# Reordering a prologue, turning the pass loop of a second product, and moving early weight splits and key/query products from GpSimd to VectorE

## The chip, the core and the metric

The kernel runs on one core of a Trainium2 chip. The metric is the device time of one execution in microseconds (us). One execution is also recorded by the hardware profiler; times "from the start" count from the start of its span. The engines are named as the profile names them: PE (TensorE) with its weight loads PEld, DVE (VectorE), ACT (ScalarE), POOL (GpSimd), and SP, whose queue issues most of the DMAs.

## The reference

What is computed is a gated linear attention over 4 batches, 8 heads, 768 tokens and head size 48, then a mixture of 4 experts over the 3072 tokens, then a gated product layer:

```python
f = 1.0 / (1.0 + np.exp(-f_logit))
for t in range(S):
    state = f[:, :, t, :, None] * state + np.einsum('bhd,bhe->bhde', k[:, :, t], v[:, :, t])
    y[:, :, t] = np.einsum('bhd,bhde->bhe', q[:, :, t], state)
...
p = domain_probs / (domain_probs.sum(-1, keepdims=True) + 1e-09)
for e in range(E):
    h = np.maximum(x @ w1[e], 0.0)
    out += p[:, e:e + 1] * (h @ w2[e])
...
a = x @ w1
b = x @ w2
h = a * b @ w3
return (h @ w_out).astype(np.float32)
```

## The kernel before, in words

**High and low parts.** Matrix products are made in a reduced format (fp32r) three times over: each operand is split into a high part and a low part, and high times high, high times low and low times high are added up in PSUM. `PASSES = ((0, 0), (0, 1), (1, 0))` lists these pairs as (part of the weight, part of the other operand); 0 is high, 1 is low.

**Units.** The expert stage works on pieces called units here: one slice f of 128 of an expert's 1024 hidden features, for one block of tokens. `stage1` makes the hidden slice: nine matmuls into `hps` (L721), the high part of `hid` on ACT (L727), the low part on DVE (L728), which reads ACT's result. `stage2` multiplies the slice with the second weight: nine matmuls into `y` (L755), three output tiles t times three passes; before, t is the outer loop and the pass the inner one. Tile t lies in a PSUM bank of its own. `stage2` of a unit runs after `stage1` of the next. After an expert's last slice DVE multiplies `y` with the gate `pb` (L771, or L774 into `tmp`, which POOL adds to `acc`, L775). The first expert is done on two half blocks of 256 tokens, so units 0 to 15 have matmuls of 256 columns; from unit 16 on they have 512, and 384 in the last layer (the M stage), where no attention is left.

**Weights.** A weight piece of 128 x 768 is loaded by SP into `raw` (L161), copied to the high part of `w` on ACT (L174), and its low part is made on POOL (L175). `feed` does this ahead of the units that need the piece. 160 pieces are split so.

**Attention.** Tokens come in 24 chunks m of 128. Step by step: `a_exp`, `a_add` (gates, L233 and L238 on ACT, from chunk 4 on L240 on DVE), `a_scan` (L245, DVE, into `pi`), `a_ln` and `a_rec` (L253, L257, ACT, into `r`), `a_k` (key times `pi`, L262: DVE for m < 3, else POOL), `a_t` (L268, DVE, on `pi` and `r`), `a_q1` (query times `r`, L275: DVE for m < 3, else POOL), `a_q2` (L279 and L282, DVE), `a_p` (PE: `psk` L311 and `ps` L319; `asb` on DVE, L322), `a_st` and `a_y` (PE: `psy` L343 to L359, `psu` L369), `a_xh` and `a_xl` (L388 on ACT, L392 on DVE: the token block `x` for the experts), and `a_s` (`us` L413 on DVE, `state` L414 on POOL).

**What sets the order.** The order of instructions on each engine is the order in which the program issues them. The prologue is a list written out by hand (`asteps`), with `warm(n)` putting in matmuls whose result nobody reads. The gates of the experts (`gate_`, L131 to L134 on DVE; `gate_rows_`, a transpose `pT` on PE, a copy `pt` on ACT and a store `pdr`) stand in that list; `load_gate(0, 0)` follows the list and reads `pdr` back into `pb`. After it, the steps of later chunks are spread over the units by due times (`plan`).

Of the kernel before, what the change touches and what calls it, by code (L numbers as in the profile page):

```python
# [8 lines left out]
F32 = mybir.dt.float32  # L9
# [3 lines left out]
ALU = mybir.AluOpType  # L13
# [7 lines left out]
PASSES = ((0, 0), (0, 1), (1, 0))  # L21
# [3 lines left out]
def gated_linear_attention_moe_kernel(  # L25
# [16 lines left out]
    nc = tc.nc  # L42
    B, H, S, D = fkq.shape[0], 2 * fkq.shape[1], fkq.shape[4], fkq.shape[2] // 2
    NT, DM = out.shape
    E = w1.shape[0]
# [100 lines left out]
    def load_gate(b, e):  # L146
        t = two.tile([128, CB, 128], F32, tag="pb", name="pb")
        src = pdr[b * CB:(b + 1) * CB, e, :]
        nc.sync.dma_start(out=t, in_=src.unsqueeze(0).to_broadcast([128, CB, 128]))
        pb[b, e] = t  # L150
# [4 lines left out]
    wts = {}  # L155
# [15 lines left out]
    def split_chunk(key, c):  # L171
        raw = raw_q.pop(c)
        w = wp.tile([128, 2, 768], F32R, tag="w", name="w")
        nc.scalar.activation(out=w[:, 0], in_=raw, func=AF.Copy)  # L174
        nc.gpsimd.tensor_tensor(out=w[:, 1], in0=raw, in1=w[:, 0].bitcast(F32), op=ALU.subtract)  # L175
        wts[key] = w


# [79 lines left out]

    def a_k(m, g=ALL):
        pi, k = part(m, "pi", None, g), kq_of(m, 0, g)  # L260
        eng = nc.vector if m < 3 else nc.gpsimd
        eng.tensor_tensor(out=k, in0=k, in1=pi[:, :, 1:], op=ALU.mult)  # L262
        nc.gpsimd.tensor_copy(out=pends[:, m, g[0]:g[1]].unsqueeze(2), in_=pi[:, :, C:])  # L263

# [6 lines left out]

    def a_q1(m, g=ALL):
        r, q = part(m, "r", None, g), kq_of(m, 1, g)
        eng = nc.vector if m < 3 else nc.gpsimd
        eng.tensor_tensor(out=q, in0=q, in1=r, op=ALU.mult)  # L275

    def a_q2(m, g=ALL):
# [199 lines left out]
    def gate_rows_():  # L477
        gate_rows(praw[0])
# [9 lines left out]
        (a_scan, 1, G0), (a_scan, 1, G1), (a_p, 0), (a_ln, 1, G0), (a_rec, 1, G0), (a_ln, 1, G1), (a_rec, 1, G1),  # L488
        (load_f, 1), (load_kq, 1), (load_v, 2), (warm, 5), (a_y, 0), (a_k, 1, G0), (a_t, 1, G0), (a_q1, 1, G0),
        (a_q2, 1, G0), (a_k, 1, G1), (a_t, 1, G1), (a_q1, 1, G1), (a_q2, 1, G1), (a_xh, 0), (a_s, 0), (warm, 5),  # L490
        (a_p, 1), (a_st, 1), (feed_, 1), (a_xl, 0), (warm, 3), (a_y, 1), (a_exp, 2), (a_add, 2), (feed_, 1), (a_scan, 2),
        (gate_,), (a_xh, 1), (a_xl, 1), (gate_rows_,), (a_ln, 2), (a_rec, 2), (a_s, 1), (warm, 5), (a_k, 2), (a_t, 2), (a_q1, 2),
        (a_q2, 2), (feed_, 1),
    ]

    def ahead(m):
# [150 lines left out]
    start = {}  # L647
# [54 lines left out]
    yps = {}  # L702
# [37 lines left out]
    def stage2(i):  # L740
        kind, sb, e, blk, f, t0, t1 = units[i]
        hb = 2 * sb + blk
        nt = t1 - t0
        h = hid.pop(i)
        w = wts[(run_of(sb, e, blk), "2", e, f // 2) if kind == "E" else (sb, "w", 0, f // 2)]
        w = w.rearrange("p l (i c) -> p l i c", i=2)[:, :, f % 2, :]
        f0 = 0 if kind == "E" else e * NF // 2
        f1 = NF - 1 if kind == "E" else (e + 1) * NF // 2 - 1
        for t in range(3):
            if f == f0:  # L750
                yps[t] = ps_y.tile([128, 512], F32, tag=f"y{t}", name="y")[:, 0:nt]
            ts = slice(t * 128, (t + 1) * 128)
            for n, (wl, hl) in enumerate(PASSES):
                lhsT, rhs = (w[:, wl, ts], h[:, hl]) if kind == "E" else (h[:, hl, ts], w[:, wl])
                nc.tensor.matmul(  # L755
                    yps[t], lhsT=lhsT, rhs=rhs, start=(f == f0 and n == 0), stop=(f == f1 and n == 2)
                )
        if f != f1:
            return
        fresh = (kind, hb, t0) not in begun  # L760
        begun.add((kind, hb, t0))
        if fresh and t0 == 0:
            n = TB if kind == "E" else NB
            acc[hb] = accp.tile([128, 3, TB], F32, tag="acc", name="acc")[:, :, 0:n]
        a = acc[hb]
        if kind == "E":
            pe = pb[hb, e].rearrange("p i t -> p (i t)")[:, t0:t1]
            for t in range(3):
                at_ = a[:, t, t0:t1]
                if fresh:  # L770
                    nc.vector.tensor_tensor(out=at_, in0=yps[t], in1=pe, op=ALU.mult)  # L771
                else:
                    tmp = two.tile([128, TB], F32, tag="tmp", name="tmp")[:, 0:nt]
                    nc.vector.tensor_tensor(out=tmp, in0=yps[t], in1=pe, op=ALU.mult)  # L774
                    nc.gpsimd.tensor_tensor(out=at_, in0=at_, in1=tmp, op=ALU.add)  # L775
            if e == E - 1:
                nc.sync.dma_start(out=x2d[:, :, hb * TB:(hb + 1) * TB], in_=a)
        else:
            for t in range(3):
                if e == 0:  # L780
                    nc.scalar.activation(out=a[:, t], in_=yps[t], func=AF.Copy)
                else:
                    nc.vector.tensor_tensor(out=a[:, t], in0=yps[t], in1=a[:, t], op=ALU.add)
                    r0 = hb * NB + t * 128
                    nc.sync.dma_start(out=out[r0:r0 + 128, :], in_=a[:, t])
# [55 lines left out]
    def feed(i, most):  # L841

        nonlocal nload, nsplit
        while nsplit < len(seq):
            while nload < len(seq) and nload < nsplit + RB - 2:
                load_chunk(seq[nload][1:])
                nload += 1
            if not most:
                break
            wb = WB  # L850
            if nsplit >= wb and last_use[seq[nsplit - wb]] >= i:
                break
            split_chunk(seq[nsplit], seq[nsplit][1:])
            nsplit += 1
            most -= 1

    with tc.manual_schedule():
        both = nc.sync, nc.scalar
        load_f(0, (0,), both)
        load_kq(0, (0, 1), both)  # L860
        load_f(0, (1,))
        load_v(0)
        load_kq(0, (1, 2))
        setup()
        praw.append(gate_load())
        feed(0, 0)
        load_v(1)
        warm(24)
        for st in asteps[:PRO]:
            run(st)  # L870
        load_gate(0, 0)
        for i, u in enumerate(units):
            feed(i, 1)
            while any(c not in wts for c in unit_chunks(u)):
                feed(i, 1)
            stage1(i)
            ends = i and units[i - 1][1:4] + units[i - 1][5:] != u[1:4] + u[5:]
            if ends:
                stage2(i - 1)
            half = (len(plan[i]) + 1) // 2  # L880
            for st in plan[i][:half]:
                run(st)
            if i and not ends:
                stage2(i - 1)
            for st in plan[i][half:]:
                run(st)
            kind, sb, e, blk, f = u[:5]
            if kind == "E" and f == NF // 2 and u[6] == TB:
                g = gates.index((2 * sb + blk, e)) + 1
                if g < len(gates):  # L890
                    load_gate(*gates[g])
        stage2(len(units) - 1)
# [221 lines left out]
```

## Time and profile before

| | |
|---|---|
| median of 3 runs | 1290.7 us (1290.09 to 1291.15) |
| the profiled execution | 1291.08 us, its span 1289.4 us |
| mean granted clock of PE over it | 0.993 |
| PE busy | 1260.7 us, 98% of the span |
| DVE busy | 634.9 us, 49% |
| POOL busy | 531.0 us, 41% |
| ACT busy | 427.7 us, 33% |

PE's clock has two levels, 2.4 and 1.2 GHz; a granted clock of 1.00 is the first, 0.50 the second, and a value between them is the mean over a stretch with both. In the rows below, the columns of a timeline are start, duration, engine, line, operation, operands, count, and in brackets the idle time of the engine just before, with what ended it. In a group of instructions they are line, engine, operation, operands, shapes and count, then busy time and mean ns of one, then the idle time before them.

### The profile page before, as it was taken

To read this page: it belongs to the slowest core of one execution; us is meant where nothing else is said; L and a number is where in the kernel's file an instruction comes from. 1 tells how busy PE (TensorE), PEld (TensorE's weight loads), DVE (VectorE), ACT (ScalarE), POOL (GpSimd) and SP (SyncE) were. 2 spreads that over 40 slices of the span, in tenths; PEclk is the share of its full clock that TensorE was granted. 3 is DMA by queue.
4 is the path that set the end of the run, shared out by engine and by line. 5 is a ranking of instruction groups with operands and counts; after the bars stand their busy time and mean duration, and the time that the engine had idled before them with its cause. 6 is when DMAs were issued, how large, how long until landed. Compare 5 with 4: busy or idle time off the path is not lost.

```text
span 1289.4 us, 18213 instructions
## 1 busy us (share of the span) xinstructions
PE 1260.7 (98%) x6935; PEld 1092.9 (85%) x6935; DVE 634.9 (49%) x1035; ACT 427.7 (33%) x760; POOL 531.0 (41%) x413
## 2 busy tenths in 40 slices
PE   7889999999999999999999999999999999999997
PEld 7888888888878888787888778788888999999997
DVE  7654443334465546565336766756624242332422
ACT  5434233342332323232222323324223433443431
POOL 3656345553542516354352635635433222222310
PEclk8989999999999999999999999999999999999999
DMA  7644343542635434252224422414134133231301
GB/s 197 181 146 121 98 133 101 148 125 72 170 115 134 140 105 148 81 156 82 77 80 134 121 80 87 144 56 131 55 99 129 56 94 98 91 104 55 117 1 40
DMA packets 107263, 138.74 MB, mean 108 GB/s; under 512 B 9664, under 2 KB 80672, under 8 KB 107168
## 3 DMA queue, kind: packets, MB, share of 16 engines
q1 hardware_dynamic: 106400, 137.16, 35.9%
q8 instruction: 56, 0.92, 0.3%
q10 hardware_dynamic: 768, 0.34, 0.1%
q14 instruction: 39, 0.32, 0.1%
HBM read 115.39 MB, written 14.20 MB: 101 GB/s over the span
## 4 chain that ended last, share of the span: by engine, by line
PE 88%; DVE 6%; POOL 2%; issue 2%; ACT 1%; DVEq 0%; ACTq 0%; POOLq 0%
PE hps L721 43%; PE y L755 36%; PE wps L634 3%; PE ps L319 2%; PE psy L359 2%; PE psy L343 1%; PE warm L469 1%; POOL w L175 1%; POOL acc L775 1%; PE psu L369 1%; DVE hid L728 1%; DVE dexp L553 1%; DVE pi L268 1%; DVE dexp L552 1%; PE psk L311 1%
## 5 line engine op out<-in xcount | busy, mean ns | idle before, releaser
L721 PE MATMUL hps<-x,w 128*128 128x512 f32 (+2 forms) x2952 | 648.3, 367 | 1.6 <-DVE ab L735 1.3
L721 PEld LDWEIGHTS hps<-x,w 128*128 128x128 f32 x2952 | 532.3, 189 | 75.8 <-DVE ab L735 1.6
L755 PE MATMUL y<-hid,w 128*128 128x512 f32 (+1 forms) x1800 | 443.7, 390 | 11.5 <-DVE hid L728 8.3
L175 POOL TENSOR_TENSOR w<-raw,w 128x768 fp32r<-128x768 f32 x160 | 302.9, 1895 | 293.0 <-ACT w L174 258.5
L755 PEld LDWEIGHTS y<-hid,w 128*128 128x128 f32 x1800 | 327.8, 189 | 88.8 <-DVE hid L728 12.0
L728 DVE SCALAR_TENSOR_TENSOR hid<-hps,hid 128x512 fp32r<-128x512 f32 (+1 forms) x200 | 133.6, 668 | 385.7 <-ACT hid L727 385.6
L727 ACT ACTIVATE hid<-hps 128x512 fp32r<-128x512 f32 (+1 forms) x200 | 115.6, 578 | 392.6 <-PE hps L721 392.5
L174 ACT ACTIVATE w<-raw 128x768 fp32r<-128x768 f32 x160 | 133.8, 837 | 55.2 <-PE y L755 55.2
L735 DVE TENSOR_TENSOR ab<-hps,a 128x384 f32<-128x384 f32 x64 | 35.6, 557 | 164.0 <-PE hps L721 164.0
L572 POOL TENSOR_TENSOR dman<-dman,dexp 128x384 f32<-128x384 f32 (+1 forms) x46 | 46.2, 1004 | 166.5 <-ACT dman L570 142.1
L755 PE MATMUL y<-w,hid 128*128 128x384 f32 x576 | 110.7, 337 | 0.1
L775 POOL TENSOR_TENSOR acc<-acc,tmp 128x512 f32<-128x512 f32 x54 | 71.9, 1361 | 79.0 <-DVE tmp L774 79.0
L755 PEld LDWEIGHTS y<-w,hid 128*128 128x128 f32 x576 | 100.7, 188 | 0.5 <-DVE hid L737 0.4
L570 ACT ACTIVATE dman<-dman 128x384 f32<-128x384 f32 (+1 forms) x46 | 24.0, 521 | 153.8 <-DVE dman L569 149.0
L736 ACT ACTIVATE hid<-ab 128x384 fp32r<-128x384 f32 x64 | 33.7, 526 | 115.3 <-DVE ab L735 115.3
L734 ACT ACTIVATE a<-hps 128x384 f32<-128x384 f32 x64 | 31.5, 492 | 77.5 <-PE hps L721 76.8
L737 DVE TENSOR_TENSOR hid<-ab,hid 128x384 fp32r<-128x384 f32 x64 | 35.8, 559 | 37.9 <-ACT hid L736 37.9
L414 POOL TENSOR_TENSOR state<-us,pwe 112x384 f32<-112x384 f32 x20 | 17.4, 869 | 88.3 <-DVE us L413 72.6
L774 DVE TENSOR_TENSOR tmp<-y,pb 128x512 f32<-128x512 f32 x54 | 35.5, 684 | 14.7 <-POOL acc L775 14.7
L268 DVE SCALAR_TENSOR_TENSOR pi<-pi,r 112x512 f32<-112x512 f32 (+1 forms) x26 | 33.7, 1295 | 14.8 <-POOL pends L263 13.0
L634 PE MATMUL wps<-uoh,u 128*128 128x384 f32 x192 | 38.0, 339 | 1.4 <-POOL u L620 0.9
L245 DVE TENSOR_TENSOR_SCAN pi<-ft,capt 112x516 f32<-112x516 f32 (+1 forms) x26 | 35.7, 1378 | 4.2 <-ACT ft L238 3.9
(87 smaller groups left out, 829.6 us busy)
## 6 DMA issues: line engine op xcount, KB each, us to landing
raw<-in_w_dram SPq DMA_DIRECT2D x112, 384.0 KB, 4.1
raw<-in_u_dram SPq DMA_DIRECT2D x27, 384.0 KB, 3.6
vt<-in_vp_dram SPq DMA_DIRECT2D x24, 288.0 KB, 4.2
pb<-pdr SPq DMA_DIRECT2D x24, 256.0 KB, 4.7
raw<-u1d SPq DMA_DIRECT2D x16, 384.0 KB, 3.2
raw<-u2d SPq DMA_DIRECT2D x16, 384.0 KB, 3.3
raw<-wdr SPq DMA_DIRECT2D x16, 384.0 KB, 3.4
x<-yr SPq DMA_DIRECT2D x80, 72.0 KB, 2.8
```

Source lines behind the costliest of these rows:

```text
L174: nc.scalar.activation(out=w[:, 0], in_=raw, func=AF.Copy)
L175: nc.gpsimd.tensor_tensor(out=w[:, 1], in0=raw, in1=w[:, 0].bitcast(F32), op=ALU.subtract)
L245: nc.vector.tensor_tensor_scan(out=pi.rearrange("p n t -> p (n t)"), data0=gates_of(m, g).rearrange("p n t -> p (n t)"), data1=capt[:, g[0 ...
L268: nc.vector.scalar_tensor_tensor(out=pi, in0=pi, scalar=-1.0, in1=r, op0=ALU.mult, op1=ALU.mult)
L572: nc.gpsimd.tensor_tensor(out=out, in0=s, in1=t.bitcast(F32), op=ALU.mult)
L634: nc.tensor.matmul(wps[ft], lhsT=w[:, a, i * 128:(i + 1) * 128], rhs=uoh[g // (NF // 2)][:, g % (NF // 2), b], start=(g == 0 and n == 0), ...
L721: nc.tensor.matmul(ps, lhsT=w[:, wl, j, fs], rhs=x[:, xl, j, t0:t1], start=(n == 0), stop=(n == 3 * KD - 1))
L727: nc.scalar.activation(out=h[:, 0], in_=prods[0], func=AF.Relu)
L728: nc.vector.scalar_tensor_tensor(out=h[:, 1], in0=prods[0], scalar=0.0, in1=h[:, 0].bitcast(F32), op0=ALU.max, op1=ALU.subtract)
L737: nc.vector.tensor_tensor(out=h[:, 1], in0=ab, in1=h[:, 0].bitcast(F32), op=ALU.subtract)
L755: nc.tensor.matmul(yps[t], lhsT=lhsT, rhs=rhs, start=(f == f0 and n == 0), stop=(f == f1 and n == 2))
L775: nc.gpsimd.tensor_tensor(out=at_, in0=at_, in1=tmp, op=ALU.add)
```

## The change

It does four things.

1. In the hand-written prologue the attention scan of chunk 2 and its logarithm and reciprocal move behind the token parts of chunk 1 (`a_xh`, `a_xl`), the gate normalization moves behind the state step of chunk 1, one `warm(5)` becomes `warm(8)` and moves ahead, and the transposition and store of the gates (`gate_rows_`) and the first load of them (`load_gate(0, 0)`) move into the unit loop, ahead of unit 1.
2. In `stage2` the pass becomes the outer loop and the tile t the inner one, and the order of the passes becomes high-high, low weight times high hidden, high weight times low hidden. In the last slice of an expert (f == f1) t stays outside, with the new order of passes inside.
3. The low parts of the 3rd to the 20th weight piece are made on DVE instead of POOL.
4. The products of `a_k` and `a_q1` are on DVE for m < 8 instead of m < 3. The small copy `pends` (L263) stays on POOL.

```diff
-        nc.gpsimd.tensor_tensor(out=w[:, 1], in0=raw, in1=w[:, 0].bitcast(F32), op=ALU.subtract)
+        eng = nc.vector if 2 <= len(wts) < 20 else nc.gpsimd
+        eng.tensor_tensor(out=w[:, 1], in0=raw, in1=w[:, 0].bitcast(F32), op=ALU.subtract)
...
-        eng = nc.vector if m < 3 else nc.gpsimd
+        eng = nc.vector if m < 8 else nc.gpsimd
...
-        (a_p, 1), (a_st, 1), (feed_, 1), (a_xl, 0), (warm, 3), (a_y, 1), (a_exp, 2), (a_add, 2), (feed_, 1), (a_scan, 2),
-        (gate_,), (a_xh, 1), (a_xl, 1), (gate_rows_,), (a_ln, 2), (a_rec, 2), (a_s, 1), (warm, 5), (a_k, 2), (a_t, 2), (a_q1, 2),
-        (a_q2, 2), (feed_, 1),
+        (a_p, 1), (a_st, 1), (feed_, 1), (a_xl, 0), (warm, 3), (a_y, 1), (a_exp, 2), (a_add, 2),
+        (feed_, 1), (a_xh, 1), (a_xl, 1), (warm, 8), (a_scan, 2), (a_ln, 2), (a_rec, 2), (a_s, 1), (gate_,), (a_k, 2),
+        (a_t, 2), (a_q1, 2), (a_q2, 2), (feed_, 1),
...
-        for t in range(3):
-            if f == f0:
+
+        passes = list(enumerate(((0, 0), (1, 0), (0, 1))))
+        order = [(t, n, p) for n, p in passes for t in range(3)]
+        if f == f1:
+            order = [(t, n, p) for t in range(3) for n, p in passes]
+        for t, n, (wl, hl) in order:
+            if f == f0 and n == 0:
                 yps[t] = ps_y.tile([128, 512], F32, tag=f"y{t}", name="y")[:, 0:nt]
             ts = slice(t * 128, (t + 1) * 128)
-            for n, (wl, hl) in enumerate(PASSES):
-                lhsT, rhs = (w[:, wl, ts], h[:, hl]) if kind == "E" else (h[:, hl, ts], w[:, wl])
-                nc.tensor.matmul(
-                    yps[t], lhsT=lhsT, rhs=rhs, start=(f == f0 and n == 0), stop=(f == f1 and n == 2)
-                )
+            lhsT, rhs = (w[:, wl, ts], h[:, hl]) if kind == "E" else (h[:, hl, ts], w[:, wl])
+            nc.tensor.matmul(yps[t], lhsT=lhsT, rhs=rhs, start=(f == f0 and n == 0), stop=(f == f1 and n == 2))
...
-        load_gate(0, 0)
         for i, u in enumerate(units):
+            if i == 1:
+                gate_rows_()
+                load_gate(0, 0)
```

Line numbers of the changed kernel lie one higher from L176 on, and five higher behind `stage2`. Three places show what moves.

On PE, right behind the `psu` matmuls of chunk 1, where the expert units begin (`hps` is unit 0, `psk` and `ps` are chunk 2), there stands before:

```order
L139 MATMUL pT<-ident,praw 96x128
L469 MATMUL warm<-cmask,ident 128x128 x5
L721 MATMUL hps<-x,w 128x256 x9
L311 MATMUL psk<-ident,kq 128x112 x4
L319 MATMUL ps_441<-kq 128x128
```

and now:

```order
L470 MATMUL warm<-cmask,ident 128x128 x8
L722 MATMUL hps<-x,w 128x256 x9
L312 MATMUL psk<-ident,kq 128x112 x4
L320 MATMUL ps_437<-kq 128x128
L320 MATMUL ps_438<-kq 128x128
```

The transposition `pT`, which reads the normalized gates, no longer stands ahead of the warm matmuls and unit 0; it comes behind the eight `ps` matmuls.

On PE, the second product of unit 2 (three tiles, with their buffer numbers), before:

```order
L721 MATMUL hps_557<-x_288,w_403 128x256 x9
L755 MATMUL y_483<-hid_503,w_410 128x256 x3
L755 MATMUL y_487<-hid_503,w_410 128x256 x3
L755 MATMUL y_491<-hid_503,w_410 128x256 x3
L721 MATMUL hps_600<-x_288,w_454 128x256 x9
```

and now:

```order
L722 MATMUL hps_560<-x_288,w_401 128x256 x9
L760 MATMUL y_486<-hid_506,w_406 128x256
L760 MATMUL y_488<-hid_506,w_406 128x256
L760 MATMUL y_490<-hid_506,w_406 128x256
L760 MATMUL y_486<-hid_506,w_406 128x256
L760 MATMUL y_488<-hid_506,w_406 128x256
L760 MATMUL y_490<-hid_506,w_406 128x256
L760 MATMUL y_486<-hid_506,w_406 128x256
L760 MATMUL y_488<-hid_506,w_406 128x256
L760 MATMUL y_490<-hid_506,w_406 128x256
L722 MATMUL hps_603<-x_288,w_457 128x256 x9
```

Neighbouring matmuls now go to different tiles, and the last three, instead of the second, fifth and eighth, are those that read the low part of `hid`.

On DVE, units 9 to 14 (the `hid` rows are the low parts of the hidden slices, `xsum` is a check sum over the block), before:

```order
L728 SCALAR_TENSOR_TENSOR hid<-hps,hid 128x256
L245 SCALAR_TENSOR_TENSOR pi<-ft,capt 112x516
L728 SCALAR_TENSOR_TENSOR hid<-hps,hid 128x256 x3
L268 SCALAR_TENSOR_TENSOR pi<-pi,r 112x4x128
L428 TENSOR_REDUCE xsum<-x 128x1
L728 SCALAR_TENSOR_TENSOR hid<-hps,hid 128x256
L322 TENSOR_TENSOR asb<-ps_945,cmask 128x512
```

and now:

```order
L176 TENSOR_TENSOR w<-raw,w 128x768
L729 SCALAR_TENSOR_TENSOR hid<-hps,hid 128x256
L263 TENSOR_TENSOR kq<-kq,pi 112x4x128
L176 TENSOR_TENSOR w<-raw,w 128x768
L729 SCALAR_TENSOR_TENSOR hid<-hps,hid 128x256
L269 SCALAR_TENSOR_TENSOR pi<-pi,r 112x4x128
L429 TENSOR_REDUCE xsum<-x 128x1
L176 TENSOR_TENSOR w<-raw,w 128x768
L729 SCALAR_TENSOR_TENSOR hid<-hps,hid 128x256
L323 TENSOR_TENSOR asb<-ps_948,cmask 128x512
```

A split `w` now stands on DVE straight ahead of nearly every `hid`, and the key product ahead of `pi`; the same instructions are gone from POOL's order.

## Rows read from the trace of the kernel before

**Rows 1.** The page, part 1: busy time of each engine.

```profile
PE 1260.7 (98%) x6935; PEld 1092.9 (85%) x6935; DVE 634.9 (49%) x1035; ACT 427.7 (33%) x760; POOL 531.0 (41%) x413
```

**Rows 2.** Busy by stretch: us, PE, PEld, DVE, ACT, POOL, PE's clock, DMA, GB/s.

```profile
50.00:60.00 10.00, 7.97 (x57) 7.42 (x57) 6.35 (x7) 3.69 (x8) 6.92 (x6) 0.83 0.11 40
80.00:90.00 10.00, 6.57 (x34) 6.58 (x34) 6.33 (x10) 2.19 (x4) 4.21 (x4) 0.66 0.19 70
```

**Rows 3.** Waits of PE, whole span: us in total, times, longest.

```profile
PE y L755 <- DVE hid L728: 8.3, 8, 4.0
```

**Rows 4.** The same view, the first 100 us alone.

```profile
PE y L755 <- DVE hid L728: 5.1, 2, 4.0
```

**Rows 5.** Timeline of PE where the units begin.

```profile
26.80 0.45 PE L139 MATMUL pT<-ident,praw 128*96 128x128 f32 x1 [4.45 <-DVE us L413]
...
31.67 1.16 PE L319 MATMUL ps<-kq 48*128 48x128 f32 x16
```

**Rows 6.** Groups of instructions on DVE, 22 to 64 us.

```profile
L245 DVE TENSOR_TENSOR_SCAN pi<-ft,capt 112x516 f32<-112x516 f32 x3 | 5.5, 1821 | 0.1
L268 DVE SCALAR_TENSOR_TENSOR pi<-pi,r 112x512 f32<-112x512 f32 x3 | 4.7, 1582 | 5.3 <-POOL pends L263 3.8 <-ACT r L257 1.5
L728 DVE SCALAR_TENSOR_TENSOR hid<-hps,hid 128x256 fp32r<-128x256 f32 x8 | 3.4, 420 | 6.5 <-ACT hid L727 6.5
L240 DVE TENSOR_SCALAR ft<-ft 112x512 f32<-112x512 f32 x1 | 2.8, 2802 | 0.0
...
L262 DVE TENSOR_TENSOR kq<-kq,pi 112x512 f32<-112x512 f32 x1 | 0.7, 683 | 0.0
```

**Rows 7.** Timeline: two of these instructions on DVE while POOL is idle.

```profile
66.59 0.42 DVE L240 TENSOR_SCALAR ft<-ft 112x512 f32<-112x512 f32 x1
...
67.72 1.22 DVE L245 TENSOR_TENSOR_SCAN pi<-ft,capt 112x516 f32<-112x516 f32 x1
```

**Rows 8.** One line's view, L268: shortest, median and longest ns, first and last start.

```profile
L268 DVE SCALAR_TENSOR_TENSOR pi<-pi,r x26: 418/688/7111, 7.6 to 649.3; 112x512 f32<-112x512 f32 x22, 112x256 f32<-112x256 f32 x4
```

**Rows 9.** Timeline, units 13 to 16.

```profile
74.19 3.62 POOL L175 TENSOR_TENSOR w<-raw,w 128x768 fp32r<-128x768 f32 x2
...
74.27 7.11 DVE L268 SCALAR_TENSOR_TENSOR pi<-pi,r 112x512 f32<-112x512 f32 x1
...
79.02 1.81 POOL L175 TENSOR_TENSOR w<-raw,w 128x768 fp32r<-128x768 f32 x1
...
83.43 2.08 PE L755 MATMUL y<-hid,w 128*128 128x256 f32 x8 [4.02 <-DVE hid L728]
...
91.66 2.33 PE L721 MATMUL hps<-x,w 128*128 128x512 f32 x9
```

**Rows 10.** Busy by stretch: up to unit 7's second product, and to unit 16.

```profile
22.00:64.00 42.00, 33.57 (x283) 31.32 (x278) 28.27 (x45) 19.15 (x41) 25.18 (x21) 0.88 0.56 168
64.00:91.66 27.66, 23.64 (x201) 22.93 (x200) 17.21 (x22) 10.65 (x19) 16.84 (x12) 0.88 0.56 163
```

**Rows 11.** The page, part 5: a DVE subtraction with both inputs in SBUF.

```profile
L737 DVE TENSOR_TENSOR hid<-ab,hid 128x384 fp32r<-128x384 f32 x64 | 35.8, 559 | 37.9 <-ACT hid L736 37.9
```

**Rows 12.** Groups of instructions on POOL, 22 to 92 us.

```profile
L175 POOL TENSOR_TENSOR w<-raw,w 128x768 fp32r<-128x768 f32 x16 | 31.0, 1946 | 10.5 <-ACT w L174 9.9 <-DMA ft<-in_fkq_dram 0.5
L275 POOL TENSOR_TENSOR kq<-kq,r 112x512 f32<-112x512 f32 x3 | 4.3, 1441 | 0.0
```

**Rows 13.** Timeline of PE, two products of 512 columns in turn.

```profile
604.00 2.24 PE L721 MATMUL hps<-x,w 128*128 128x512 f32 x9
...
606.08 2.26 PE L755 MATMUL y<-hid,w 128*128 128x512 f32 x9
...
608.18 1.09 PE L721 MATMUL hps<-x,w 128*128 128x512 f32 x4
```

**Rows 14.** Timeline at an expert's end: DVE's third `tmp`, PE's next `y`.

```profile
595.94 0.69 DVE L774 TENSOR_TENSOR tmp<-y,pb 128x512 f32<-128x512 f32 x1 [0.81 <-POOL acc L775]
...
596.54 2.26 PE L755 MATMUL y<-hid,w 128*128 128x512 f32 x9
```

More of the change, by code (lines that the diff above doesn't have):

```diff
@@ L273, in a_q1 @@
         r, q = part(m, "r", None, g), kq_of(m, 1, g)
-        eng = nc.vector if m < 3 else nc.gpsimd
+        eng = nc.vector if m < 8 else nc.gpsimd
         eng.tensor_tensor(out=q, in0=q, in1=r, op=ALU.mult)
```

## The prediction, made before the changed kernel was run

> **What bounds the kernel now.** I read the busy times first. PE is busy for 1260.7 of 1289.4 us [rows 1], so all that any edit can win is the 28.7 us in which PE is idle, and the time in which it runs at the lower of its two clock levels. The view by stretches shows where that is: between 50 and 60 us the mean granted clock is 0.83, between 80 and 90 us 0.66 [rows 2]; from 100 us on PE is nearly always busy at 1.00. The list of PE's waits gives the cause: the second product waits eight times for the low part of the hidden slice from DVE, 8.3 us in all, of which 5.1 us fall in the first 100 us [rows 3, 4]. One more wait there, 4.45 us, stands ahead of the gate transposition `pT` [rows 5]. The reader is to see a kernel bound by PE everywhere but in its first 92 us, where DVE paces it.
>
> Why is DVE late, though busy for half the time? The groups of 22 to 64 us show instructions of one shape at several times their usual duration: the scan L245 at 1.82 us on average against 1.22 us when POOL is idle, L240 at 2.80 against 0.42, L268 at 1.58 against a median of 0.69 [rows 6 to 8]. The worst stands in unit 13: L268 takes 7.11 us, and all through it POOL works on splits and a query product without a gap [rows 9]. So DVE stands still behind POOL, and PE stands behind DVE: 4.02 us later in the same rows.
>
> The Trainium skill, "SBUF — State Buffer", section "Who interferes with whom", says that a DVE instruction with two inputs in SBUF and a GpSimd instruction that reads SBUF exclude each other for a whole instruction, and that the order of issue decides. By that, L268 would lose one POOL instruction at most, and the stall would be some 2 us; the row shows a wait through four in turn, so the measurement decides and the stall counts in full.
>
> **The sum, part by part.** The profiled execution took 1291.08 us, 0.4 us above the median shown; I sum against it.
>
> *Front, up to 64 us (parts 1, 3 and 4).* PE's order changes only a little there: the DVE chain sets when its work comes. DVE is busy for 28.3 of the 42 us from 22 to 64 [rows 10]. Of that, stalls behind POOL are 3 x (1.82 - 1.22) = 1.8, 3 x (1.58 - 0.69) = 2.7 and 2.80 - 0.42 = 2.4, together 6.9 us; they go, since the splits and products behind which DVE stood are no longer on POOL. Added on DVE are eight splits (the 3rd to the 10th piece), four products of 0.68 us (chunks 3 and 4) [rows 6], and the scan of chunk 2, 1.2 us, which moves from just before this stretch into it. A split on DVE is not in the trace. The nearest rows are the subtraction of 384 columns, 0.559 us [rows 11], and the product of 512, 0.683 us [rows 6]: 0.124 us for 128 columns more, so 0.683 + 2 x 0.124 = 0.93 us for 768. Its bounds are 0.68 us, the shorter row, and 1.95 us, what the same split takes on POOL [rows 12]; I take 0.93 because operation and engine are those of the near rows. Added: 8 x 0.93 + 4 x 0.68 + 1.2 = 11.4 us. DVE then has 28.3 - 6.9 + 11.4 = 32.8 us of work where it spends 42 now. Its idle time is 42 - 28.3 = 13.7 us. Of this, 3.8 us are L268 waiting for the `pends` copy, which stood on POOL behind the key product, and vanish [rows 6]; 9.9 us remain, among them 6.5 us in which the low part waits for ACT's high part [rows 6], and a split now stands straight ahead of nearly every such low part, so it runs inside that wait: 5 waits x 0.93 = 4.7 us. Left idle are 5.2 us, and the stretch takes 32.8 + 5.2 = 38.0, **4.0 us less**. Bounds: if no added work fits into the waits, 32.8 + 9.9 = 42.7, a loss of 0.7; if all of it fits, a gain of 9.2.
>
> That holds the reordered list too. `pT` no longer stands ahead of the units, so its wait of 4.45 us is not PE's any more; but what is late next is `ps` of chunk 2, which now starts at 31.67 [rows 5] and needs the query products behind the scan, gate and key steps on DVE. So I do not add the 4.45 us; they are inside the 4.0. The three more warm matmuls fill time in which PE has nothing else. In the SP queue, the store of the gates and the load behind it now stand behind four weight loads and two loads of v, and ahead of one weight load and the gate and key loads of chunks 4 and 5. The queue stands until ACT has made `pt`, some 4 us later than now; those loads feed work that comes over 10 us later, which covers it. If that cover is gone, chunk 4 is late by up to those 4 us.
>
> *Units 8 to 15, 64 to 91.66 us (parts 3 and 4).* L268 goes from 7.11 to 0.69 us, so PE's wait of 4.02 us in unit 13 goes [rows 9]. With it goes the half clock that follows: a mean of 0.66 over 10 us is 6.8 us at the lower level, of which 5.7 us are work from 83.43 us on; half of it, **2.8 us**, comes back. Does the added DVE work fit? DVE has 17.2 us busy [rows 10], less 6.4 of stall, plus 7 splits of 0.93 and two products of 0.68: 18.7 us. PE needs 27.7 - 4.0 - 2.8 = 20.9 us for the same units. It fits, with 2.2 us to spare: **6.8 us less**. Bounds: with splits of 1.26 us the margin is gone; with 1.95 us DVE would need 25.8, and the gain is 1.9.
>
> *The second product from 100 us on (part 2).* Six waits for the low part are left there, 8.3 - 5.1 = 3.2 us [rows 3, 4]. Now six matmuls instead of one go ahead of the first that reads it. Nine take 2.10 us [rows 13], so the low part is needed 5 x 0.233 = 1.17 us later; the waits average 0.5 us: **3.2 us less**; bounds 0 and 3.2. What it could cost is the change of tile at every matmul. The product with two changes of tile takes 2.10 us, the first product with none 2.08 [rows 13]: at most 0.01 us each. At that bound six more in some 200 units would cost 12 us; but 2.10 against 2.08 is the resolution of the rows, so I take 0. A second price: at an expert's start, tile 3 is touched after two matmuls instead of six. DVE's third `tmp` ends at 595.94 + 0.69 = 596.63, PE would now touch the tile at 596.54 + 0.47 = 597.01 [rows 14]; 0.4 us of slack are left, so nothing.
>
> After about 130 us the other three parts end; POOL's relief there frees nothing PE waits for.
>
> Sum: 4.0 + 6.8 + 3.2 = 14.0 us, so 1291.1 - 14.0 = **1277 us**.
>
> **The rivals.**
>
> *DVE's chain eats the front.* If ACT's waits stay whole, the front gives -0.7 and a new gap of PE ahead of chunk 2's `ps` may bring the half clock once more, 1.7 us as between 50 and 60 [rows 2]. With 6.8 and 3.2 the time is 1291.1 - 7.6 = 1283.5 us. For it: the whole added work stands in DVE's order before PE's needs. Against it: splits stand where DVE waits now.
>
> *More comes back.* If all added work hides, the front gives 9.2: 1291.1 - 19.2 = 1272 us. For it: 13.7 us of idle DVE; against it: ACT's order is the same as before.
>
> *The moved work is as slow on DVE as on POOL, slower in the end.* This is one mechanism: the two engines share the way to SBUF, and a split takes 1.95 us, a product 1.44, wherever it runs [rows 12]. Then the front adds 8 x 1.02 + 4 x 0.76 = 11.2 us and turns from 4.0 to -7.2; units 8 to 15 add 7 x 1.02 + 2 x 0.76 = 8.7, less the 2.2 spare, so 6.8 turns to 0.3; with 3.2 the time is 1291.1 + 3.7 = 1295 us. It decides from about four fifths of the way between my prices and POOL's. Against it: the DVE rows of the same kind at 0.56 and 0.68 us. The Trainium skill, "Perfetto Trace Analysis", section "Optimizing Scalar/DVE Operations", warns that moving work between these two engines might not help, because they share a port to SBUF; the stalls of L268 agree with the sharing, the short DVE rows speak against the price.
>
> *Changing banks costs clock.* If the change of bank at every matmul let PE fall to the lower level for even 4% of the span, 52 us, half of that would be lost: 1277 + 26 = 1303 us. Against it: PE changes banks at two of nine already, with a level clock. The Trainium skill, "TensorE: Matmul & The Clock Gate", section "A second HAM failure mode: psum-queue depth-cycling", reports a kernel that cycled through banks in which small gaps brought the clock down; no row here shows such gaps.
>
> *Nothing happens.* If DVE's lateness is only moved, the three gains cancel against new waits: 1290 us.
>
> **How the numbers follow.** Forecast 0.62, the front eaten 0.16, more back 0.09, slow on DVE 0.06, clock 0.02, nothing 0.05. 0.2% of the time, 2.6 us, is about what a measurement of this kernel can tell from no change. So faster 0.62 + 0.16 + 0.09 = 0.87, same 0.05, slower 0.08. The range goes from 1271, just past the third case, to 1286, past the second with a part of the late gain missing; that leaves out the last three cases and little else.
>
> **What would show it.** Right, step by step: L268 in unit 13 near 0.7 us and splits on DVE near 0.9; no wait of several us for `hid` in the first 100 us; unit 16's `hps` starting at 81 us instead of 91.66; the front's part seen in unit 7's second product at 60 to 61 instead of 64.6; no waits of `y` for the low part after 100 us; nine matmuls of the second product still at 2.10 us. Wrong: splits near 1.9 us; PE waiting for `hid` or `ps` in many units; a granted clock below 1 after 100 us; unit 16 later than 86 us.

## The result and the profile after

The changed kernel takes 1278.7 us (median of 4 runs, 1278.27 to 1279.05) where the kernel before, on the same chip in the same session, takes 1290.9 (1290.09 to 1291.43). The ratio is 0.9906, with a 95% interval of 0.9892 to 0.992: faster by 0.8 to 1.1%. 1277 us was forecast, with 1271 to 1286 as the range. The profiled execution of the changed kernel took 1278.84 us, with a span of 1277.1 us and a mean granted clock of 0.996.

The page's part 1, against [rows 1], shows what moved from one engine to the other: POOL has 42 us less, DVE only 9 us more.

```profile
PE 1256.6 (98%) x6941; PEld 1089.6 (85%) x6941; DVE 643.6 (50%) x1063; ACT 427.5 (33%) x760; POOL 488.5 (38%) x385
```

The waits of PE over the whole span (us in total, times, longest) answer to [rows 3]:

```profile
PE psk L312 <- issue: 3.3, 1, 3.3
...
PE ps L320 <- DVE kq L280: 1.5, 1, 1.5
...
PE y L760 <- DVE hid L729: 1.2, 1, 1.2
...
PE y L760 <- DVE acc L774: 0.4, 1, 0.4
```

The 8.3 us for the low part have shrunk to 1.2, and the 4.45 us ahead of `pT` [rows 5] are gone. New are a gap of 3.3 us ahead of `psk` and 1.5 us ahead of `ps`, both of chunk 2, which make up for `pT`'s wait, and 0.4 us for DVE's `acc`. L774 is the product of `y` with the gate, L771 before: from there to the unit loop the lines lie three higher, not five.

The same stretches as in [rows 2], and the one from 30 to 40 us (us, PE, PEld, DVE, ACT, POOL, PE's clock, DMA, GB/s):

```profile
30.00:40.00 10.00, 9.70 (x65) 9.48 (x66) 7.41 (x12) 4.52 (x9) 1.90 (x2) 0.66 0.36 96
50.00:60.00 10.00, 8.93 (x83) 8.15 (x82) 7.73 (x13) 5.52 (x13) 0.39 (x2) 1.00 0.27 90
80.00:90.00 10.00, 10.00 (x78) 8.60 (x77) 5.61 (x11) 3.01 (x6) 0.56 (x1) 1.00 0.21 60
```

The clock of 50 to 60 and of 80 to 90 us is back at 1.00. Now it is low between 30 and 40 us: PE spends some 6 us there at the lower level, on matmuls that count.

PE's timeline (start, duration, engine, line, operation, count, and in brackets the idle time before) gives the two events by which the prediction measured itself, unit 7's second product and the first product of unit 16:

```profile
62.23 1.22 PE L760 MATMUL y<-hid,w 128*128 128x256 f32 x9
...
82.37 2.37 PE L722 MATMUL hps<-x,w 128*128 128x512 f32 x9
```

Against 64.64 and 91.66 us they are 2.4 and 9.3 us earlier. DVE in units 9 to 14, against [rows 9]:

```profile
66.62 0.83 POOL L264 COPY pends<-pi 112x4 f32<-112x4 f32 x1 [3.46 <-DVE pi L246]
...
68.65 0.96 DVE L176 TENSOR_TENSOR w<-raw,w 128x768 fp32r<-128x768 f32 x1 [0.92 <-ACT w L174]
...
71.79 0.68 DVE L269 SCALAR_TENSOR_TENSOR pi<-pi,r 112x512 f32<-112x512 f32 x1
```

The instruction of 7.11 us now takes 0.68, and a split on DVE takes 0.96. DVE's groups of 22 to 64 us, against [rows 6]:

```profile
L176 DVE TENSOR_TENSOR w<-raw,w 128x768 fp32r<-128x768 f32 x8 | 7.5, 954 | 3.7 <-ACT w L174 3.5
L729 DVE SCALAR_TENSOR_TENSOR hid<-hps,hid 128x256 fp32r<-128x256 f32 x9 | 3.8, 421 | 2.6 <-ACT hid L728 2.6
L246 DVE TENSOR_TENSOR_SCAN pi<-ft,capt 112x516 f32<-112x516 f32 x3 | 3.7, 1231 | 0.1
...
L269 DVE SCALAR_TENSOR_TENSOR pi<-pi,r 112x512 f32<-112x512 f32 x3 | 2.1, 693 | 0.4
...
L241 DVE TENSOR_SCALAR ft<-ft 112x512 f32<-112x512 f32 x1 | 0.9, 880 | 0.0
```

The scan is down from 1821 to 1231 ns, `pi` from 1582 to 693, and the wait for `pends` (3.8 us) is gone.

### The profile page after: what moved, and what is told of

Its sections match the earlier page's. It is cut to its first block, busy times and chain, and to the rows that moved or that the text cites. A ratio compares the mean times of both kernels' runs of the same rounds, so it can differ in the third digit from the quotient of the medians.

```text
span 1277.1 us, 18201 instructions
## 1 busy us (share of the span) xinstructions
PE 1256.6 (98%) x6941; PEld 1089.6 (85%) x6941; DVE 643.6 (50%) x1063; ACT 427.5 (33%) x760; POOL 488.5 (38%) x385
## 4 chain that ended last, share of the span: by engine, by line
PE 89%; DVE 4%; DMA 2%; ACT 1%; POOL 1%; issue 1%; SPq 0%; DVEq 0%; ACTq 0%
PE hps L722 44%; PE y L760 37%; PE wps L635 3%; PE ps L320 2%; PE psy L360 2%; PE psy L344 1%; DMA vt<-in_vp_dram 1%; PE psu L370 1%; POOL acc L778 1%; ACT w L174 1%; PE psk L312 0%; DMA raw<-in_w_dram 0%; DMA ft<-in_fkq_dram 0%; ACT hid L728 0%; DVE dexp L554 0%
## 5 line engine op out<-in xcount | busy, mean ns | idle before, releaser
L176 POOL TENSOR_TENSOR w<-raw,w 128x768 fp32r<-128x768 f32 x142 | 267.8, 1887 | 287.2 <-ACT w L174 258.6
L286 POOL TENSOR_TENSOR pwe<-pw,hm 112x8 f32<-112x8 f32 (+1 forms) x26 | 9.8, 379 | 85.9 <-DVE pw L283 85.9
L635 PEld LDWEIGHTS wps<-uoh,u 128*128 128x128 f32 x192 | 34.1, 188 | 4.2 <-POOL u L621 1.4
```

Source lines behind the costliest of these rows:

```text
L176: eng.tensor_tensor(out=w[:, 1], in0=raw, in1=w[:, 0].bitcast(F32), op=ALU.subtract)
L635: nc.tensor.matmul(wps[ft], lhsT=w[:, a, i * 128:(i + 1) * 128], rhs=uoh[g // (NF // 2)][:, g % (NF // 2), b], start=(g == 0 and n == 0), ...
```

## Where the 12 us come from

Profiles of one and the same prologue start its first chunks up to half a microsecond apart (`ps` of chunk 1 starts at 16.80 and at 16.29 us in the last two versions below, which do not differ up to there). So I cut every trace at four events on PE, and compare the pieces:

- `ps` of chunk 1, the last step that no version touches;
- unit 7's second product;
- unit 16's first product;
- the last group of second products.

Pieces in us, each the difference of two starts; the median time is that of the run's own comparison, in which the kernel before takes 1290.4 to 1290.9:

| version | median | ratio, 95% interval | `ps` 1 to unit 7 | unit 7 to 16 | unit 16 to last |
|---|---|---|---|---|---|
| before | 1290.9 | | 47.51 | 27.02 | 1187.12 |
| changed | 1278.7 | 0.9906, 0.9892 to 0.992 | 45.69 | 20.14 | 1184.90 |
| 2 alone (e1) | 1287.5 | 0.9975, 0.9964 to 0.9986 | 47.20 | 25.17 | 1184.86 |
| 3, 4 (e2) | 1279.5 | 0.9915, 0.99 to 0.993 | 43.31 | 20.14 | 1187.16 |
| 1 alone (e3) | 1290.5 | 0.9999, 0.999 to 1.0009 | 46.91 | 26.95 | 1187.18 |
| 1, 3, 4 (e4) | 1281.7 | 0.9933, 0.992 to 0.9947 | 44.66 | 20.13 | 1187.23 |
| 3 alone (e5) | 1280.2 | 0.9915, 0.9902 to 0.9929 | 46.19 | 20.11 | 1187.10 |
| 4 alone (e6) | 1284.2 | 0.9947, 0.9934 to 0.9961 | 47.72 | 20.11 | 1187.14 |
| 2, 3, 4 (e10) | 1277.4 | 0.9895, 0.988 to 0.9911 | 43.65 | 20.14 | 1184.92 |
| changed, gap filled (e8) | 1277.2 | 0.9894, 0.9879 to 0.9909 | 44.28 | 20.13 | 1184.95 |
| changed, scan first (e12) | 1275.6 | 0.9889, 0.9873 to 0.9906 | 41.94 | 20.13 | 1184.89 |
| e12, gap filled (e13) | 1275.9 | 0.9885, 0.9869 to 0.9902 | 41.93 | 20.13 | 1185.03 |
| e13, first slice (e14) | 1275.3 | 0.9884, 0.9867 to 0.99 | 41.93 | 20.13 | 1184.91 |

Of the 12.3 us between the two spans, 1.82 + 6.88 + 2.22 = 10.9 us lie in these pieces. The other 1.4 are the start (`ps` 1 at 16.54 instead of 17.13) and what comes after the last group (9.83 instead of 10.62). That last stretch lies between 9.25 and 11.6 us over all profiles, without order, so I don't credit it to the change. Many intervals of the ratios overlap; what sets neighbouring versions apart below is the pieces, and it is one profile each. The profiled execution lies within 0.7 us of its version's median, except in e5 (1282.39 us, 2.2 above it and the longest of five) and e10 (1278.73 us, 1.35 above it and the longest of four).

## The experiments: the parts one by one

**e1: part 2 alone**, on the kernel before.

```diff
+        passes = list(enumerate(((0, 0), (1, 0), (0, 1))))
+        order = [(t, n, p) for n, p in passes for t in range(3)]
+        if f == f1:
+            order = [(t, n, p) for t in range(3) for n, p in passes]
...
```

> The kernel before with the new order of passes alone. Theory of the prediction (three separate gains): the six waits of the second product for the low part after 100 us go, 3.2 us; in the first 100 us each such wait shrinks by five matmuls of 0.12 us, so about 1 us more; unit 16 still starts at about 90.5 us, since DVE still stands behind POOL. Sum: 4 us less than before, about 1286.5. Rival (the pass order is what brings nearly all): 8 us less or more, 1283 or below, and unit 16 before 86 us.

Measured: 1287.5 us, a gain of 3.2 where I had some 4; the theory holds, and unit 16 starts at 89.74 us. From unit 16 on 2.26 us are gained, and 1.85 between units 7 and 16, where the late low part is needed later. In that last piece the pass order is worth its own 2.2 to 2.3 us whatever else is changed: every version with it has 1184.9 to 1185.0 in the last piece, every one without it 1187.1 to 1187.2.

**e2: parts 3 and 4**, the splits and the products on DVE, on the kernel before. The last pair of lines stands in `a_k` and in `a_q1`.

```diff
-        nc.gpsimd.tensor_tensor(out=w[:, 1], in0=raw, in1=w[:, 0].bitcast(F32), op=ALU.subtract)
+        eng = nc.vector if 2 <= len(wts) < 20 else nc.gpsimd
+        eng.tensor_tensor(out=w[:, 1], in0=raw, in1=w[:, 0].bitcast(F32), op=ALU.subtract)
...
-        eng = nc.vector if m < 3 else nc.gpsimd
+        eng = nc.vector if m < 8 else nc.gpsimd
```

> The kernel before with the 18 splits and the key and query products of chunks 3 to 7 on DVE alone. Theory: the 7.11 us instruction and PE's wait of 4.02 us behind it go with the half clock, 6.9 us between units 7 and 16; the front gives 0 to 4; the waits after 100 us stay at about 3 us. Sum 7 to 11 us less than before, 1280 to 1284. Rival (pass order brings nearly all): at most 3 us less. Rival (DVE gets too much and slows the front): unit 7's second product later than the 64.6 us of before, and the total within 3 us of before.

Measured: 1279.5 us, 11.1 less than before and a little more than I had given: nearly all of the gain. The front is shorter by 4.20 us and units 7 to 16 by 6.88.

**e3: part 1 alone**, the reordered prologue on the kernel before.

```diff
-        (a_p, 1), (a_st, 1), (feed_, 1), (a_xl, 0), (warm, 3), (a_y, 1), (a_exp, 2), (a_add, 2), (feed_, 1), (a_scan, 2),
-        (gate_,), (a_xh, 1), (a_xl, 1), (gate_rows_,), (a_ln, 2), (a_rec, 2), (a_s, 1), (warm, 5), (a_k, 2), (a_t, 2), (a_q1, 2),
-        (a_q2, 2), (feed_, 1),
+        (a_p, 1), (a_st, 1), (feed_, 1), (a_xl, 0), (warm, 3), (a_y, 1), (a_exp, 2), (a_add, 2),
+        (feed_, 1), (a_xh, 1), (a_xl, 1), (warm, 8), (a_scan, 2), (a_ln, 2), (a_rec, 2), (a_s, 1), (gate_,), (a_k, 2),
+        (a_t, 2), (a_q1, 2), (a_q2, 2), (feed_, 1),
...
-        load_gate(0, 0)
         for i, u in enumerate(units):
+            if i == 1:
+                gate_rows_()
+                load_gate(0, 0)
```

> The kernel before with the reordered prologue and the gates behind unit 0 alone. Theory: 0 to 3 us less than before, 1288 to 1291, with the long L268 and PE's wait of 4 us behind it still there. Rival (the reordering brings most): 8 us less or more.

Measured: 1290.5 us, no difference. Inside it two things cancel: from `ps` 1 to chunk 2's `psy` PE takes 22.19 us instead of 20.01, and from there to unit 7 24.72 instead of 27.50. PE comes later to a place where it waited for DVE before: its wait of 1.11 us for the low part in unit 3 is gone, and the granted clock of 50 to 60 us is 1.00 instead of 0.83.

**e4: parts 1, 3 and 4**: the changed kernel with the old pass order.

> The changed kernel with the old order of passes. Theory: the waits after 100 us are back, 3 to 4 us, so 1282 to 1283, with unit 16 at 82 to 83.5 us as in the changed kernel. Rival (pass order brings nearly all): 1287 or more.

Measured: 1281.7 us, a little below what I expected, and 2.1 more than e2, which has the old prologue. Here the times show it too: the five runs of e4 took 1280.97 us or more, the four of e2 1280.63 or less. The front is 1.35 us longer. With DVE on time, the reorder has less left to cancel against.

**e5: part 3 alone**, the first hunk of e2's diff.

> The kernel before with part 3 alone: 18 low parts on DVE, the products stay on POOL. My theory: the splits are most of what held DVE up (31.0 of POOL's busy time from 22 to 92 us), so this alone brings 8 to 10 of the 11.1 us of parts 3 and 4: 1281 to 1283 us, the L268 of unit 13 at 0.7 to 2.2 us (one query product of 1.44 us may still stand before it). Rival: any POOL work in a row is enough, and chunks 3 to 7 are still late because key and query products stay on POOL behind the copy pends: 1285 us or more, L268 still over 3 us.

Measured: 1280.2 us. As forecast the splits alone carry most of it; it is even below the 1281 to 1283 that I gave, and by time it can't be told from both parts together (the ratio is 0.9915 in e2 and here). The `pi` of unit 13 takes 0.68 us. For the front this profile is a poor guide: it is the longest of the five executions, with a mean granted clock of 0.995 where the other four had 0.997 or 0.998, and PE's clock in it is 0.87 from 30 to 40 us and 0.83 from 50 to 60, against 0.99 and 1.00 in e2.

**e6: part 4 alone**, the second hunk.

> The kernel before with part 4 alone: the key and query products of chunks 3 to 7 on DVE, all splits stay on POOL. My theory: POOL's row of splits stays, so L268 of unit 13 still waits for three of them, 5.4 us instead of 7.1, and the products themselves may be held up too: a gain of 1 to 3 us, 1287.7 to 1289.7 us, the granted clock between 80 and 90 us still below 0.85. Rival: the products were the tie between the two engines (DVE waits for POOL's product, then for its port), and the gain is over 5 us: below 1285.5 us. Third: DVE is held up more often and it is slower, over 1291 us.

Measured: 1284.2 us, so my theory fell and the rival's time came true. All splits are still on POOL, and units 7 to 16 still take 20.11 us, as in every version with either part. The timeline of e6 at the place of [rows 9]:

```profile
73.72 1.84 POOL L175 TENSOR_TENSOR w<-raw,w 128x768 fp32r<-128x768 f32 x1
74.36 1.76 DVE L268 SCALAR_TENSOR_TENSOR pi<-pi,r 112x512 f32<-112x512 f32 x1
75.59 2.21 POOL L175 TENSOR_TENSOR w<-raw,w 128x768 fp32r<-128x768 f32 x1
```

The first POOL split ends at 75.56. DVE's `pi` ends at 76.12, 0.56 us later, which is nearly its usual 0.69, and the second split takes 2.21 us instead of 1.84. This reads as DVE waiting through the first split and then going ahead of the second. In the kernel before, the same instruction waited through four POOL instructions. So it isn't the amount of work on POOL alone that makes the long wait. Why DVE gets in between two splits here and not there stays open. What is shown: either part alone takes away the 6.9 us of units 7 to 16, and the products alone bring nothing in the front. What the splits alone bring there stays open: 1.32 us in e5's profile, against 4.20 with both parts, but e5's median gain of 10.4 us less 6.9 would leave some 3.5.

## The experiments: what the reorder costs

**e10: parts 2, 3 and 4**, the changed kernel with the old prologue (e3's diff backwards).

> The changed kernel with the old order of the prologue (parts 2, 3 and 4 alone). My theory, after the first four runs: the reorder costs about 2 us once the other parts are in, because PE then meets a gap ahead of the first matmuls of chunk 2 and runs at the lower clock after it. Then the gains of pass order (3.2) and of the work moved to DVE (11.1) add up: 1290.7 - 14.3 = 1276.4 us, unit 16 starts at about 80 us, and PE's wait of 4.5 us for the gate transposition is still there. Rival: the reorder is worth nothing either way and the difference between the runs without and with it was chance: 1278.7 us, as the changed kernel. Third: the gains of the two parts overlap: 1278.5 us or more with unit 16 at 80 us all the same, and waits for hid after 100 us as before.

Measured: 1277.4 us, between my 1276.4 and the rival's 1278.7, with unit 16 at 81.20 us. The front is 2.04 us shorter than in the changed kernel. By time alone the two are not apart (0.988 to 0.9911 against 0.9892 to 0.992), and the two profiled executions are 0.1 us apart: e10 comes to `ps` 1 0.87 us later and spends 1.05 us more behind the last group. By the pieces they are apart, as e2 and e4 are by time, and the rows say where. PE in the changed kernel from the end of unit 0's first product on:

```profile
28.19 0.57 PE L312 MATMUL psk<-ident,kq 112*128 112x112 f32 x4 [3.33 <-issue]
30.30 2.08 PE L320 MATMUL ps<-kq 48*128 48x128 f32 x16 [1.53 <-DVE kq L280]
32.31 0.45 PE L139 MATMUL pT<-ident,praw 128*96 128x128 f32 x1
32.41 2.27 PE L722 MATMUL hps<-x,w 128*128 128x256 f32 x9
34.48 2.12 PE L760 MATMUL y<-hid,w 128*128 128x256 f32 x9
...
38.74 1.04 PE L344 MATMUL psy<-kq,state 112*96 112x128 f32 x8
```

PE in e10, with the old prologue:

```profile
27.08 0.45 PE L139 MATMUL pT<-ident,praw 128*96 128x128 f32 x1 [4.46 <-DVE us L414]
27.33 2.34 PE L470 MATMUL warm<-cmask,ident 128*128 128x128 f32 x10
29.32 2.27 PE L722 MATMUL hps<-x,w 128*128 128x256 f32 x9
...
32.10 1.16 PE L320 MATMUL ps<-kq 48*128 48x128 f32 x16
33.19 1.34 PE L722 MATMUL hps<-x,w 128*128 128x256 f32 x9
34.37 1.23 PE L760 MATMUL y<-hid,w 128*128 128x256 f32 x9
...
37.57 1.04 PE L344 MATMUL psy<-kq,state 112*96 112x128 f32 x8
```

Counted from `ps` 1, the reorder does bring chunk 2's `ps` earlier, by 0.93 us (30.30 - 16.54 = 13.76 against 32.10 - 17.41 = 14.69). From there to `psy` PE then needs 8.44 us instead of 5.47, since `ps`, `hps` and `y` run at the lower level: 2.08 us against 1.16, 2.27 against 1.34, 2.12 against 1.23. In the old order the half clock after the gap falls on warm matmuls and unit 0; in the new one the warm matmuls and unit 0 stand ahead of the gap, and it falls on work behind it. 2.97 - 0.93 = 2.04 us.

**e8: the gap filled.** Sixteen more warm matmul pairs on PE behind unit 0's first product.

```diff
+            if i == 0:
+                warm(16)
```

> The changed kernel with sixteen more warm matmuls on PE straight after the first product of unit 0, in the gap ahead of the first matmuls of chunk 2 (3.3 us idle there, half clock from 30.3 to 36.4 us). Theory A (the half clock is what the reorder costs): the clock between 30 and 40 us rises from 0.66 to above 0.9, unit 7's second product starts 1.5 to 3 us earlier, and the time is 1276 to 1277.5 us. Theory B (DVE's chain of chunk 2, with the gate steps ahead of the key product, sets when PE can go on): the clock rises but PE waits longer for chunk 2's ps and the time stays at 1278.7 within 0.6 us. Theory C: the extra matmuls run past the gap and push everything behind them: 1279.5 or more.

Measured: 1277.2 us, a front 1.41 us shorter. That is theory A, though less than it said: the front gains a little under its 1.5 to 3 us, and the granted clock of 30 to 40 us is 0.83, not above 0.9. The windows of e8 show it at 1.00 up to 32 us, then at half level after all, behind the remaining wait of 1.48 us for chunk 2's `kq`:

```profile
30.00:32.00 2.00, 1.45 (x19) 1.33 (x20) 2.00 (x4) 0.41 (x2) 1.35 (x1) 1.00 0.00 0
32.00:34.00 2.00, 2.00 (x13) 2.00 (x12) 2.00 (x5) 1.38 (x3) 0.37 (x1) 0.60 0.10 25
34.00:36.00 2.00, 2.00 (x12) 2.00 (x11) 2.00 (x3) 0.00 (x0) 0.00 (x0) 0.55 0.30 73
```

**e12: the scan back.** What makes chunk 2 late is on DVE. In the changed kernel it stands idle ahead of the token part, then does the scan, and the gate steps stand ahead of the key product:

```profile
22.57 1.49 DVE L393 TENSOR_TENSOR x<-psy,x 96x384 fp32r<-96x384 f32 x4 [2.19 <-ACT x L389]
24.09 1.23 DVE L246 TENSOR_TENSOR_SCAN pi<-ft,capt 112x516 f32<-112x516 f32 x1
...
26.11 0.75 DVE L132 TENSOR_SCALAR psum__389<-psum__389 128x24 f32<-128x24 f32 x1
...
27.41 0.68 DVE L263 TENSOR_TENSOR kq<-kq,pi 112x512 f32<-112x512 f32 x1
```

```diff
-        (feed_, 1), (a_xh, 1), (a_xl, 1), (warm, 8), (a_scan, 2), (a_ln, 2), (a_rec, 2), (a_s, 1), (gate_,), (a_k, 2),
-        (a_t, 2), (a_q1, 2), (a_q2, 2), (feed_, 1),
+        (feed_, 1), (a_scan, 2), (a_xh, 1), (a_xl, 1), (warm, 8), (a_ln, 2), (a_rec, 2), (a_s, 1), (a_k, 2),
+        (a_t, 2), (a_q1, 2), (a_q2, 2), (gate_,), (feed_, 1),
```

> The changed kernel with the scan of chunk 2 back ahead of the token parts of chunk 1, where DVE waits 2.2 us for ACT, and the gate steps behind the query products of chunk 2. My theory (what makes chunk 2's ps late in the changed kernel is what the reorder put ahead of its key steps on DVE): psk starts at 26.2 to 26.8 us instead of 28.19, ps at 28 to 28.8 instead of 30.30, the wait ahead of psk shrinks from 3.3 to about 1.7 us, some half clock stays, and unit 7's second product starts at 60 to 61.2 us instead of 62.23: 1276.6 to 1277.6 us. Rival: chunk 2 is earlier but a later chunk sets unit 7 all the same (ACT stands 4.4 us waiting for the scan of chunk 4): unit 7 at 62 us, no gain, 1278.7 us within 0.6.

Measured: 1275.6 us, a front of 41.94 us, 3.75 less than in the changed kernel and more than I expected. PE in e12:

```profile
25.66 0.57 PE L312 MATMUL psk<-ident,kq 112*128 112x112 f32 x4 [0.49 <-PE hps L722]
28.49 1.16 PE L320 MATMUL ps<-kq 48*128 48x128 f32 x16 [2.25 <-DVE kq L280]
...
30.85 1.40 PE L760 MATMUL y<-hid,w 128*128 128x256 f32 x9
```

With the scan in DVE's idle time and the gates behind the products, the wait ahead of `psk` is 0.49 us instead of 3.33, and `ps` runs at full level in spite of its 2.25 us. No half clock is left: the granted clock is 1.00 from 20 to 100 us. The two moves were made together; what each is worth was not tried.

**e13: e12 with the gap filled**, by `warm(10)` at the place of e8.

> As the run before, and ten more warm matmul pairs behind the first product of unit 0 (some 2.2 us). My theory: both gap and half clock go, the granted clock between 30 and 40 us is above 0.95, unit 7's second product starts at 58 to 60 us, and the time is 1274 to 1276 us, below all versions so far. Rival: what bounds unit 7 after this is the chain of chunk 4 on ACT and DVE, so that it does not start before 61.0 us, where the two runs without the gap both stand (61.06 and 61.07), and the time stays at 1276.8 to 1277.4 us.

Measured: 1275.9 us, the front as in e12 (41.93). The time lies where I said, but not for my reason: e12 already has the full clock, so the warm matmuls have nothing to give back.

**e14: e13 with the tile outermost in an expert's first slice too.**

```diff
-        if f == f1:
+        if f == f0 or f == f1:
```

> As the run before, with the tile outermost in an expert's first slice too, as the kernel before had it. It tests the one place where part 2 cost something: in the changed kernel the second product at 734 us waits 0.36 us for DVE's acc and takes 2.99 us instead of 2.26. My theory: that product is back at 2.3 to 2.4 us without the wait, some 1.0 us comes back there, the other waits of y for hid do not return, and the time is 0.3 to 1.0 us below that of the run before. Rival: the first slices now wait for the low part again (each 0.4 to 0.5 us), so that the gain is given back: within 0.3 us of the run before, or above it.

Measured: 1275.3 us, 0.6 below e13, inside its interval. PE at the start of the expert concerned, in the changed kernel:

```profile
734.34 2.99 PE L760 MATMUL y<-hid,w 128*128 128x512 f32 x9 [0.36 <-DVE acc L774]
```

and in e14:

```profile
730.32 2.34 PE L760 MATMUL y<-hid,w 128*128 128x512 f32 x9 [0.35 <-DVE acc L774]
...
739.71 1.51 PE L635 MATMUL wps<-uoh,u 128*128 128x384 f32 x7 [0.44 <-POOL u L621]
```

The product is back at 2.34 us, but the 0.35 us ahead of it stay, and 0.44 us are lost again to a wait of `wps` for POOL's `u` behind it: the last piece is shorter by 0.12 us only. The 0.6 us are not this edit's: the profiled executions are 0.63 us apart, and 0.51 of them lie ahead of `ps` 1.

These three have the lowest medians of all versions that were run, some 15 us below the kernel before (e14: 0.9867 to 0.99 of it). They can't be told apart by time; e12 is the simplest.

## Why the prediction was right, point by point

The time came 1.7 us above the forecast, but the three terms come to 10.9 us in the traces, where I had 14.0: the other 1.4 us of the gain lie in the start and the end of the span, in none of my terms, and are luck. The middle term was right by its mechanism and its size; the front gave half of its term, the second product two thirds.

**Units 8 to 15: forecast 6.8 us, measured 6.88.** The stall went, the half clock behind it went, and PE is busy without a gap from 62.23 to 82.37 us while DVE works 17.22 of those 20.14 us; I had 18.7 of 20.9. The price of a split, 0.93 us worked out from two neighbours, came to 0.954. What the sum did not see is that either part alone would do this (e5, e6).

**The front: forecast 4.0 us, measured 1.82 between the events.** Unit 7 at 62.23 us misses the 60 to 61 that I had named. DVE from 22 us to there, against [rows 10]:

```profile
22.00:62.23 40.23, 33.73 (x281) 31.21 (x280) 32.33 (x58) 18.68 (x39) 6.11 (x9) 0.92 0.63 177
```

DVE's work is as forecast, 32.33 us against 32.8, but it stands idle for 40.23 - 32.33 = 7.9 us, where I had left 5.2. The failed step is "the three more warm matmuls fill time in which PE has nothing else", with the reorder counted as free inside the 4.0 us. `pT`'s wait of 4.45 us came back as 3.33 + 1.53 = 4.86 us ahead of chunk 2, and the half clock behind it fell on `ps` and the products of units 0 and 1. Split at chunk 2's `psy`, the front shows the two terms apart. From `psy` to unit 7 it is 27.50 us before and 62.23 - 38.74 = 23.49 now: 4.01 less, from DVE's work, since e10 with the old prologue has the same 61.06 - 37.57 = 23.49 (e2, without part 2 as well, 23.79). From `ps` 1 to `psy` it is 37.14 - 17.13 = 20.01 before and 38.74 - 16.54 = 22.20 now: 2.19 more, from the reorder (e10: 20.16). The rival "DVE's chain eats the front" had named this gap and its half clock, at 1.7 us; it came true as a part of the forecast, not in its place. Of DVE's terms the scan (1.23 us) and `pi` (0.69) came to what I had set; L241 takes 0.88, not 0.42, which is 0.5 us of the stall left. The delay in the SP queue cost nothing that shows: the store `pdr` stands at 33.09 us instead of 27.59, but from 20 to 65 us no engine's wait in the list names a load.

**The second product: forecast 3.2 us, measured 2.22.** PE's waits for the low part fall from 3.1 us behind unit 16 to 1.2. The one that is left, 0.95 us before, is there because it stands in an expert's last slice, where t stays outside and two matmuls, not six, go ahead of the first that reads the low part; the forecast had overlooked this. "0.4 us of slack are left, so nothing" was wrong at one start of an expert out of all: 0.36 us of wait and a product of 2.99 us. PE's idle time in the piece is 1187.12 - 1180.09 = 7.03 us before and 1184.90 - 1179.41 = 5.49 now; the other 0.68 us are shorter rows, whose cause I did not look for.

**The rivals.** "DVE's chain eats the front" is answered above, and "more comes back" fell with the front. "As slow on DVE as on POOL" fell: 0.954 us for a split where POOL takes 1.9. The Trainium skill, "Perfetto Trace Analysis", section "Optimizing Scalar/DVE Operations", says that moving work between these engines might not help; here it brought 11.1 us (e2). "Changing banks costs clock" fell too: the clock is 1.00 from 40 us to the last matmul, and a product of 512 columns with a change of tile at every matmul shows the 2.26 us of [rows 13]:

```profile
91.89 2.26 PE L760 MATMUL y<-hid,w 128*128 128x512 f32 x9
```

"Nothing happens" fell, but for the reorder by itself it holds (e3).

## What to carry to other kernels

Price a change of order against the kernel with the other edits in, and not against the one before: the reorder was free while DVE was late and cost 1.3 to 2.1 us once it was not. Where a gap of PE can't be closed, look at which matmuls stand behind it, since here they paid the lower clock (in e12 they did not); padding matmuls ahead of the gap did not help, behind it they took the loss. And an instruction at many times its usual duration on a half-idle engine (7.11 us against 0.69) is worth more than its own time: look for what shares its way.

## What the runs showed of the hardware that I had not expected

**POOL is held up as well.** With the work on DVE, a small instruction of POOL, 203 ns in the median, waits in its turn; the changed kernel at 30 us:

```profile
30.24 1.82 DVE L176 TENSOR_TENSOR w<-raw,w 128x768 fp32r<-128x768 f32 x2
...
30.40 1.72 POOL L286 TENSOR_TENSOR pwe<-pw,hm 112x8 f32<-112x8 f32 x1 [3.45 <-DVE pw L283]
```

It ends with the second of two DVE splits, not with the first. In the kernel before, too, the POOL split that follows on [rows 7] begins 0.78 us before the scan there ends, so POOL is idle only for the first part of that scan, and takes 2.42 us where two others in [rows 9] take 3.62 together:

```profile
68.16 2.42 POOL L175 TENSOR_TENSOR w<-raw,w 128x768 fp32r<-128x768 f32 x1 [2.59 <-ACT w L174]
```

The Trainium skill, "SBUF — State Buffer", section "Who interferes with whom", has a lock for one whole instruction: e6's `pi` behind one split agrees with it, the 1.72 us through two splits and the 7.11 us through four do not.

**A wait does not always cost the clock.** PE waited 1.48 us ahead of `ps` in e8 and ran at half level soon after; it waited 2.25 us at the same place in e12 and stayed at 1.00. What tells the two apart was not tried.
